# Turning the softmax scores of seven attention tiles by 32x32 blocks and through device memory, in a fused attention, gated-unit and soft-routing kernel

## The chip, the cores and the metric

The kernel runs on one core of a Trainium2 chip. The metric is device microseconds of one launch. Its engines here are PE (TensorE, matrix products), DVE (VectorE), ACT (ScalarE), POOL (GpSimd) and SP (SyncE, which issues the DMAs).

## The reference, cut to what matters

Three parts run behind one another on 4 batches of 576 tokens (2304 tokens, 512 features, 8 heads of 64).

```python
# attention: pooled by 4 (global) plus a band of +-3 keys (local)
scores = where(|i - j| < 4, scale * q @ k.T, -1e9)
attn = exp(scores - max); attn = attn / (sum + 1e-9)
x = out_up + attn @ v
# gated unit, 512 -> 1536 -> 512
h = sigmoid(x @ w_gate) * (x @ w_val);  x2 = h @ w_out
# soft routing: 8 experts with 4 slots each
logits = x2 @ phi
slot_input = softmax(logits, tokens).T @ x2
slot_out[e] = relu(slot_input[e] @ w1[e]) @ w2[e]
out = softmax(logits, slots) @ slot_out
```

All of it is float32. The change touches the step `attn @ v` of the local part.

## The kernel before, in words

The tokens are cut into 18 tiles of 128. Tiles 0 to 15 get their local attention on PE; tiles 16 and 17 get theirs on DVE, ACT and POOL (the functions named z_...), in a stage that opens when the on-chip memory of the first kind is given back.

Local attention of one tile (helpers from line 390 on). A tile is two blocks of 64 queries. `lsq` (L450) makes the scores of 8 heads against 70 keys for both blocks on PE, into two PSUM banks; `lmq` (L465) scales and masks them into the tile `t` (128 partitions by 8 heads by 70 keys); `lx` (L500) takes the maxima; `le` (L506) the exponentials, eight on ACT; `la` and `ln` (L514, L519) divide by the sums on DVE. `lt` (L525) turns the eight 128x70 pieces with eight identity matmuls on PE into two PSUM banks `psT`, and `lc` (L531) copies these on ACT into `pt` (70 partitions). `lo` (L537) makes 16 products of `pt` with the values `lv` on PE into `psO`; `xa` (L551) adds the global part on DVE and `l_split` (L592) splits the result into a high and a low half on ACT and POOL. `pt` has one buffer, `t` and `lv` have two.

The gated unit (`unit`, L874) of a tile has six parts of 256 hidden columns. A part is 12 matmuls of 128x512 into one of two banks `psM`, in two halves of six; ACT takes a tanh and DVE a product (`uh`, L866), which frees the bank. Tile t is worked on after its attention is done, so the attention of later tiles, the global attention and the routing of earlier tiles are laid between the halves.

The order is written by hand in half-slots (`place`, L1196): half-slot h comes after half h of the matmuls, counted from tile 4, with 12 half-slots to a tile. PE runs in this order, exactly. On the other engines, and in SP's queue, the framework orders by its own simulated times; only from half-slot 100 on is DVE held to program order as well. The attention tiles T = 6 to 15 have h = 10(T - 6): scores at h, division at h + 5, turning at h + 7, values at h + 9:

```python
        place(h + 5, lambda T=T: l_norm(T))
        place(h + 7, lambda T=T: (l_tr(T, 0), l_tr(T, 1)))
        place(h + 9, lambda T=T: (l_av(T), l_split(T)))
```

At half-slot 100 `to_band` (L1262) gives back the memory of `t`, `pt`, `lq`, `lk` and `lv`, and the rows of the last two tiles are loaded into it (`token_row`, L611); the products with them (`z_prod`, L636) stand on DVE ahead of the next `uh`.

One thing in the kernel before is already done in the way of the change: for tiles 3 to 11 the hidden values `h` are turned for the routing by `turn` (L900: four DVE transposes of 32x32 blocks, each followed by a DMA to device memory, `hod`) and `move` (L910: four DMAs back, into `hT`), at places 1 and 2 of a tile's 12 half-slots for most tiles.

The expert weights (33 MB) are loaded late, into memory that the gated unit gives back piece by piece (L1041, L1084, L1092 and, at the end, `get2` and `get2p`, L1046 and L1099, under the helper line 136 or L1047).

Of the kernel before, what the change touches and what calls it, by code (L numbers as in the profile page):

```python
# [7 lines left out]
F32 = mybir.dt.float32  # L8
# [7 lines left out]
P = 128  # L16
QB = 64
KW = QB + 6
# [4 lines left out]
def kernel(  # L23
# [16 lines left out]
    nc = tc.nc  # L40
    B, NP, _, SP = qT.shape[0], qT.shape[1], qT.shape[2], kT.shape[3]
# [5 lines left out]
    NTL = NT // P  # L47
    TS = 6
    TB = 16
    FF = wo.shape[0]  # L50
    NC = DM // P
    FU = 256
    NU = FF // FU
    NF = FF // P
    GW = FF // 4
    NE, _, F2 = w1.shape
# [3 lines left out]
    def pool(stack, name, bufs, side=None, space=None):  # L60
        kw = {"space": space} if space is not None else {}
        if side:
            kw["side"] = side
        return stack.enter_context(tc.tile_pool(name=name, bufs=bufs, **kw))
# [10 lines left out]
    sf = pool(dense, "sf", 1)  # L75
# [7 lines left out]
    def bank(pl, tag, name):  # L83
        return pl.tile([P, 512], F32, name=name, tag=tag)
# [9 lines left out]
    mask = sf.tile([P, 3, KW], F32, name="mask")  # L94

    wod = tc.dram_tile([FF, DM], F32, name="wod")
    hod = [tc.dram_tile([4 * P, GW], F32, name=f"hod{i}") for i in range(2)]

    st = {"pin": True, "pe": False, "all": False, "vec": False, "act": False}
# [8 lines left out]
    def tmm(*args, **kw):  # L108
        ins = nc.tensor.matmul(*args, **kw)  # L109
        if st["pe"]:  # L110
            tc.keep_in_program_order(ins)
# [21 lines left out]
    vec, act, gps, syn = Engine(nc.vector, "vec"), Engine(nc.scalar, "act"), Engine(nc.gpsimd, "all"), Engine(nc.sync, "all")  # L133

    def load(dst, src):
        ins = nc.sync.dma_start(dst, src)
        if st["pin"]:
            tc.keep_in_program_order(ins)
# [88 lines left out]
    def copy(alt, dst, src):  # L227
        if alt:
            vec.tensor_copy(out=dst, in_=src)
        else:  # L230
            act.copy(out=dst, in_=src)
# [155 lines left out]
    L = {}  # L387
# [44 lines left out]
    def load_tile(t):  # L432
        if t < NTL:
            load_q(t), load_k(t), load_v(t, 1)
# [15 lines left out]
    def lsq(t):  # L450
        d = L[t]
        for h in range(2):
            d["ps", h] = bank(ps_at, "at", "psS")
        for p in range(NP):
            for j in range(2):
                c = slice(64 * j, 64 * j + 64)
                ko = d["ko"][j]
                for h in range(2):
                    r = slice(64 * h, 64 * h + 64)
                    tmm(  # L460
                        d["ps", h][c, p * KW:(p + 1) * KW], lhsT=d["q"][r, p, j * QB:(j + 1) * QB],
                        rhs=d["k"][r, p, ko:ko + KW], start=True, stop=True, tile_position=(64 * h, 64 * j),
                    )

    def lmq(t, h):  # L465
        d = L[t]
        if "t" not in d:
            d["t"] = sf.tile([P, 2, NP, KW], F32, name="t", tag="t", bufs=2)
        kinds = [0 if i == 0 else (2 if i == NB - 1 else 1) for _, i in blocks(t)]
        rows = [(0, P, kinds[0])] if kinds[0] == kinds[1] else [(64 * j, 64 * j + 64, kinds[j]) for j in range(2)]  # L470
        ps = d.pop(("ps", h))
        for a, b, kind in rows:
            vec.scalar_tensor_tensor(
                out=d["t"][a:b, h],
                in0=ps[a:b, :NP * KW].rearrange("p (b w) -> p b w", w=KW),
                scalar=0.125,
                in1=mask[a:b, kind].unsqueeze(1).to_broadcast([b - a, NP, KW]),
                op0=ALU.mult,
                op1=ALU.add,
            )  # L480
# [16 lines left out]
    def groups(t):  # L497
        return L[t]["t"].rearrange("p j b w -> p (j b) w")

    def lx(t):  # L500
        d = L[t]
        mx = d["mx"] = sm.tile([P, 2 * NP], F32, name="mxl", tag="mxl")
        vec.tensor_reduce(out=mx, in_=groups(t), axis=AX.X, op=ALU.max, negate=True)
        d["sl"] = sm.tile([P, 2 * NP], F32, name="sl", tag="sl")
# [20 lines left out]
    def lt(t, j):  # L525
        d = L[t]
        ps = d["ps", j] = bank(ps_at, "at", "psT")
        for p in range(NP):
            ttr(ps[:KW, p * P:(p + 1) * P], d["t"][:, j, p, :], ident)

    def lc(t, j, alt=False):  # L531
        d = L[t]
        if "pt" not in d:
            d["pt"] = sf.tile([KW, 2, NP, P], F32, name="pt", tag="pt")
        copy(alt, d["pt"][:, j], d.pop(("ps", j))[:KW, :].rearrange("p (b q) -> p b q", q=P))

    def lo(t):  # L537
        d = L[t]
        ps = d["ps"] = bank(ps_at, "at", "psO")
        for j in range(2):  # L540
            for p in range(NP):
                for h in range(2):
                    r, c = slice(64 * h, 64 * h + 64), slice(64 * j, 64 * j + 64)
                    tmm(
                        ps[r, p * P + j * QB:p * P + (j + 1) * QB],
                        lhsT=d["v"][j][:, p * P + 64 * h:p * P + 64 * h + 64],
                        rhs=d["pt"][:, h, p, c] if t >= TS else d["pt"][:, j, p, r],
                        start=True, stop=True,
                    )

    def xa(t):  # L551
        x = new_x(t)
        pv = L[t].pop("ps").rearrange("e (p g r) -> e p g r", p=NP, r=4)
        xv = x.rearrange("e p (g r) -> e p g r", r=4)
        (b0, i0), (b1, i1) = blocks(t)
        if b0 == b1:
            pieces = [(b0, i0 * 16, 0, 32)]
        else:
            pieces = [(b0, i0 * 16, 0, 16), (b1, i1 * 16, 16, 16)]
        for b, o, g, n in pieces:  # L560
            vec.tensor_tensor(
                out=xv[:, :, g:g + n], in0=pv[:, :, g:g + n],
                in1=odb[b][:, :, o:o + n].unsqueeze(3).to_broadcast([P, NP, n, 4]), op=ALU.add,
            )
# [4 lines left out]
    def l_norm(t):  # L569
        la(t), ln(t)  # L570

    def l_tr(t, j):
        lt(t, j), lc(t, j)

    def l_av(t):
        lo(t), xa(t)
# [6 lines left out]
    def to_hi(t):  # L583
        xh[t] = xs.tile([P, NC, P], F32R, name="xh", tag="xh")
        act.copy(out=xh[t], in_=xt[t])

    def to_lo(t, eng):
        xl[t] = xs.tile([P, NC, P], F32R, name="xl", tag="xl")
        eng.tensor_tensor(out=xl[t], in0=xt.pop(t), in1=xh[t].bitcast(F32), op=ALU.subtract)
        L.pop(t, None)  # L590

    def l_split(t):  # L592
        to_hi(t), to_lo(t, gps)
# [6 lines left out]
    def pieces(m):  # L600

        a, r = TB * P + 2 * P * m, []
        while a < TB * P + 2 * P * (m + 1):
            b, o = divmod(a, S)
            n = min(S - o, TB * P + 2 * P * (m + 1) - a)
            p0 = (a - TB * P - 2 * P * m) // 2
            r.append((p0, n // 2, b, o))
# [13 lines left out]
    def z_start(m):  # L621
        d = Z[m] = {}
        ew = st["ew"]
        d["q"] = ew.tile([P, 2, DM], F32, name="zq", tag="zq")
        a = TB * P + 2 * P * m
        load(d["q"], qn[a:a + 2 * P, :].rearrange("(p r) e -> p r e", r=2))
# [86 lines left out]
    def z_rows(m, r):  # L713
        o = Z[m]["o"]
        t = TB + 2 * m + r
        ps = bank(ps_at, "at", "psT")
# [149 lines left out]
    def uh(t, u):  # L866
        if t not in hs:
            hs[t] = hs[t - 3] if TX < t < TY else (st["h5"] if t == K0 else hp).tile([P, FF], F32, name="h", tag="h")
        vec.scalar_tensor_tensor(
# [30 lines left out]
    def turn(t):  # L900
        if "y" not in st:
            st["y"] = hp.tile([P, FF], F32, name="hy", tag="h")
        src = hs[t].rearrange("p (c r w) -> p c r w", r=4, w=32)
# [207 lines left out]
    def pair(k):  # L1111
        if k not in G:
# [6 lines left out]
            out=grp, in_=ident.rearrange("p (g r) -> p g r", r=4), axis=AX.X, op=ALU.add  # L1119
# [76 lines left out]
    def place(at, fn, rank=1):  # L1196
        half_slots.setdefault(at, []).append((rank, len(half_slots.get(at, [])), fn))

    EVERY = 10
    for i, T in enumerate(range(TS, TB)):  # L1200
        h = EVERY * i
        place(
            h, lambda T=T: (load_tile(T + 1) if T + 1 < TB else None, lsq(T), lmq(T, 0), lmq(T, 1))
        )
        place(h + 1, lambda T=T: lx(T))
        for j in range(4):
            place(h + 1 + j, lambda T=T, j=j: le(T, j, 2), 2)
        place(h + 5, lambda T=T: l_norm(T))
        place(h + 7, lambda T=T: (l_tr(T, 0), l_tr(T, 1)))
        place(h + 9, lambda T=T: (l_av(T), l_split(T)))  # L1210
    for i, h in enumerate((10, 20, 45, 62)):
        q = 4 + i
        for a in range(2):
# [41 lines left out]
    for t in range(K0 + 3, TL):  # L1255
        h = HS * (t - K0)
# [30 lines left out]
    for t in range(K0, TL):  # L1287
# [7 lines left out]
        for u in range(NU):  # L1295
            h = HS * (t - K0) + 2 * u
# [69 lines left out]
    for p in PLAN:  # L1366
# [3 lines left out]
        i = "abc".index(p)  # L1370
        t, u = TL + i, un[i]
# [245 lines left out]
    t = 0  # L1617
# [55 lines left out]
```

## Time and profile before

| what | value |
|---|---|
| runs, median of 3 | 541.03 us (540.21 to 541.84) |
| the profiled execution's own time | 541.66 us |
| its span, first to last instruction | 539.9 us |
| busy PE / DVE / ACT / POOL | 509.8 / 289.9 / 225.6 / 93.2 us |
| mean granted clock of TensorE | 0.994 of full speed |
| moved by DMA | 108.57 MB |

The span is 1.8 us shorter than the execution's own time, and the execution is 0.6 us above the median. In the rows further on, times are microseconds from the span's start. A row of the chain gives start, duration and the work that the end of the span goes back to. A row of the timeline gives start, duration, engine, line, operation, output and inputs, and in brackets the idle time of the engine before it. Operations recorded by helpers carry the helper's line (L109 and L114 for PE, L126 for the others, L136 for loads). One float32 product counts as two or more MATMULs in some groups.

### The profile page before, as it was taken

To read this page: it belongs to the slowest core of one execution; us is meant where nothing else is said; L and a number is where in the kernel's file an instruction comes from. 1 tells how busy PE (TensorE), PEld (TensorE's weight loads), DVE (VectorE), ACT (ScalarE), POOL (GpSimd) and SP (SyncE) were. 2 spreads that over 40 slices of the span, in tenths; PEclk is the share of its full clock that TensorE was granted. 3 is DMA by queue.
4 is the path that set the end of the run, shared out by engine and by line. 5 is a ranking of instruction groups with operands and counts; after the bars stand their busy time and mean duration, and the time that the engine had idled before them with its cause. 6 is when DMAs were issued, how large, how long until landed. Compare 5 with 4: busy or idle time off the path is not lost.

```text
span 539.9 us, 11054 instructions
## 1 busy us (share of the span) xinstructions
PE 509.8 (94%) x4218; PEld 375.3 (70%) x4218; DVE 289.9 (54%) x667; ACT 225.6 (42%) x773; POOL 93.2 (17%) x154
## 2 busy tenths in 40 slices
PE   3989999999999999999999999999999999999972
PEld 2566777788877767777777777777777777753431
DVE  6989999888326563645353544458763211241123
ACT  3887646476445443433353442413333212231222
POOL 0210322001344142312220101000284000000000
PEclk9999999999999999999999999999999999999997
DMA  8897665887534557744751514295216666799948
GB/s 305 244 258 266 188 232 191 275 266 240 160 118 118 150 165 218 194 114 126 165 153 48 157 42 118 81 294 191 83 56 254 240 254 227 240 398 343 387 151 333
DMA packets 68332, 108.57 MB, mean 201 GB/s; under 512 B 10744, under 2 KB 32632, under 8 KB 68280
## 3 DMA queue, kind: packets, MB, share of 16 engines
q1 hardware_dynamic: 68280, 107.88, 61.6%
q8 instruction: 33, 0.54, 0.4%
q14 instruction: 19, 0.16, 0.1%
HBM read 92.91 MB, written 14.94 MB: 200 GB/s over the span
## 4 chain that ended last, share of the span: by engine, by line
PE 76%; DMA 11%; DVE 7%; ACT 2%; issue 1%; SPq 1%; DVEq 0%; ACTq 0%
PE psM L109 51%; PE psL L109 6%; DMA ew<-in_w_dram 5%; PE psO L109 4%; DVE wf L126 3%; PE psH L114 2%; PE psS L109 2%; PE psT L114 2%; PE psW L109 2%; PE psD L109 1%; PE psEH L109 1%; DMA g<-in_kT_dram 1%; DMA raw<-in_wg_dram 1%; DMA raw<-in_wv_dram 1%; DMA lv<-in_vp_dram 1%
## 5 line engine op out<-in xcount | busy, mean ns | idle before, releaser
L109 PE MATMUL psM<-whi,xh 128*128 128x512 f32 x432 | 182.8, 423 | 2.0 <-DVE h L126 2.0
L109 PE MATMUL psM<-wlo,xh 128*128 128x512 f32 x432 | 170.6, 395 | 0.0
L109 PE MATMUL psM<-whi,xl 128*128 128x512 f32 x432 | 170.6, 395 | 0.0
L126 ACT ACTIVATE th<-psM 128x256 f32<-128x256 f32 x108 | 41.3, 383 | 155.7 <-PE psM L109 151.8
L109 PEld LDWEIGHTS psM<-whi,xh 128*128 128x128 f32 x432 | 81.5, 189 | 32.1 <-issue 9.8
L126 DVE SCALAR_TENSOR_TENSOR h<-th,psM 128x256 f32<-128x256 f32 x108 | 44.7, 414 | 102.5 <-ACT th L126 102.3
L109 PEld LDWEIGHTS psM<-whi,xl 128*128 128x128 f32 x432 | 81.2, 188 | 19.5
L109 PEld LDWEIGHTS psM<-wlo,xh 128*128 128x128 f32 x432 | 81.6, 189 | 13.7
L126 DVE SCALAR_TENSOR_TENSOR wf<-raw,wf 128x512 uint32<-128x512 uint32 x72 | 48.5, 686 | 0.3
L126 ACT ACTIVATE t<-t,mxl 128x70 f32<-128x70 f32 x128 | 43.4, 348 | 10.9 <-DVE mxl L126 10.9
L126 POOL TENSOR_TENSOR xl<-x,xh 128x512 fp32r<-128x512 f32 x15 | 19.8, 1320 | 129.3 <-ACT xh L126 129.3
L126 ACT ACTIVATE wf<-raw 128x512 f32<-128x512 f32 x36 | 24.3, 676 | 25.8 <-DMA raw<-in_wg_dram 11.1
L126 POOL TENSOR_TENSOR wlo<-wf,whi 128x512 fp32r<-128x512 f32 x10 | 14.8, 1487 | 67.9 <-ACT whi L126 31.1
L126 ACT ACTIVATION_READ_ACCUMULATOR t<-t,mxl 128x1 f32 x128 | 24.9, 194 | 0.0
L126 DVE SCALAR_TENSOR_TENSOR t<-psS,mask 128x280 f32<-128x280 f32 (+1 forms) x38 | 16.0, 443 | 16.5 <-PE psS L109 16.3
L126 ACT COPY hT<-psH 128x512 f32<-128x512 f32 (+1 forms) x29 | 16.1, 556 | 13.5 <-PE psH L114 13.1
L126 ACT CAST xh<-x 128x512 fp32r<-128x512 f32 x18 | 11.2, 623 | 21.3 <-DVE x L126 21.3
L689 POOL TENSOR_TENSOR hy<-hy,prv 128x512 f32<-128x512 f32 x12 | 17.1, 1459 | 7.2 <-PE psM L109 3.8
L109 PEld LDWEIGHTS psO<-pt,lv 70*64 70x64 f32 x448 | 14.2, 138 | 6.0 <-issue 4.3
L126 DVE STREAM_TRANSPOSE hy<-h 128x384 f32<-128x384 f32 x36 | 17.8, 548 | 0.5 <-DMA hod<-hy 0.3
L126 DVE TENSOR_SCALAR wf<-wf 128x512 uint32<-128x512 uint32 x36 | 15.4, 437 | 4.5 <-ACT wf L126 4.4
L109 PE MATMUL psO<-pt,lv 70*64 70x64 f32 x448 | 16.1, 225 | 1.6 <-DMA lv<-in_vp_dram 1.2
(195 smaller groups left out, 693.0 us busy)
## 6 DMA issues: line engine op xcount, KB each, us to landing
ew<-in_w_dram SPq DMA_DIRECT2D x19, 1024.0 KB
hod<-hy SPq DMA_DIRECT2D x36, 192.0 KB
hT<-hod SPq DMA_DIRECT2D x36, 192.0 KB
raw<-in_wg_dram SPq DMA_DIRECT2D x12, 512.0 KB
raw<-in_wv_dram SPq DMA_DIRECT2D x12, 512.0 KB
raw<-in_wo_dram SPq DMA_DIRECT2D x12, 512.0 KB
ewp<-in_w_dram SPq DMA_DIRECT2D x20, 256.0 KB
ewp<-in_w_dram SPq DMA_DIRECT2D x8, 512.0 KB
```

The lines of the kernel that those rows point to most:

```text
L109: ins = nc.tensor.matmul(*args, **kw)
L114: ins = nc.tensor.transpose(*args)
L126: ins = fn(*args, **kw)
L689: nc.gpsimd.tensor_tensor(out=e, in0=e, in1=pr[:, r], op=ALU.add)
```

## The change

For tiles 9 to 15 the eight identity matmuls and the two ACT copies go. In their place stands `l_turn`: three DVE transposes of 32x32 blocks (key columns 0 to 31, 32 to 63 and 38 to 69 of all eight heads, 128x256 elements each), one DMA of the result to device memory (128 rows of 3 KB), and three DMAs back into `pt`, in runs of 1 KB onto 32, 32 and 6 partitions. The result's buffer `py` takes the memory of tile 4's hidden values. `pt` keeps its size but has another layout, so that `lo` reads two runs of 32 columns instead of one of 64. `l_turn` stands at h + 5, right behind the division (tile 9: h + 8), and the values at h + 10 (tile 9: h + 14) instead of h + 9. All of tile 15 comes two half-slots earlier (88 instead of 90), so its values are at 98 instead of 99.

```diff
+    TURNED = (9, 15)
+    pod = [tc.dram_tile([P, 24 * 32], F32, name=f"pod{i}") for i in range(2)]
+    def l_turn(t):
+        d = L[t]
+        if t < 9:
+            y = st["y"]
+        else:
+            if "py" not in st:
+                st["py"] = st["h5"].tile([P, FF], F32, name="py", tag="h")
+            y = st["py"]
+        y = y[:, :24 * 32]
+        yv = y.rearrange("p (k g w) -> p k g w", g=2 * NP, w=32)
+        g = groups(t)
+        vec.transpose(out=yv[:, 0], in_=g[:, :, :32])
+        vec.transpose(out=yv[:, 1], in_=g[:, :, 32:64])
+        vec.transpose(out=yv[:, 2], in_=g[:, :, KW - 32:])
+        m = pod[t % 2]
+        nc.sync.dma_start(m, y)
+        pt = sf.tile([KW, 4, 2 * NP, 32], F32, name="pt", tag="pt")
+        d["pt"] = pt
+        mv = m.rearrange("(a w) (k e) -> k w a e", w=32, k=3)
+        for k, r, w in ((0, 0, 0), (1, 32, 0), (2, 64, 96 - KW)):
+            nc.sync.dma_start(pt[r:r + 32 - w].rearrange("w a g q -> w a (g q)"), mv[k, w:])
...
-                        rhs=d["pt"][:, h, p, c] if t >= TS else d["pt"][:, j, p, r],
+                        rhs=(
+                            d["pt"][:, 2 * j:2 * j + 2, h * NP + p, :] if TURNED[0] <= t <= TURNED[1]
+                            else d["pt"][:, h, p, c] if t >= TS else d["pt"][:, j, p, r]
+                        ),
...
-        h = EVERY * i
+        h = min(EVERY * i, 88)
...
-        place(h + 7, lambda T=T: (l_tr(T, 0), l_tr(T, 1)))
-        place(h + 9, lambda T=T: (l_av(T), l_split(T)))
+        if TURNED[0] <= T <= TURNED[1]:
+            w = h + {7: 10, 8: 8, 9: 8}.get(T, 5)
+            place(w, lambda T=T: l_turn(T))
+            place(h + {7: 14, 8: 12, 9: 14}.get(T, 10), lambda T=T: (l_av(T), l_split(T)))
+        else:
+            place(h + 7, lambda T=T: (l_tr(T, 0), l_tr(T, 1)))
+            place(h + 9, lambda T=T: (l_av(T), l_split(T)))
```

## Rows read from the trace of the kernel before

**Rows 1.** The page: busy time and share of the span by engine.

```profile
PE 509.8 (94%) x4218; PEld 375.3 (70%) x4218; DVE 289.9 (54%) x667; ACT 225.6 (42%) x773; POOL 93.2 (17%) x154
```

**Rows 2.** Busy time by stretch: start:end, length, then PE, PEld, DVE, ACT, POOL, clock, DMA.

```profile
294.00:314.00 20.00, 20.00 (x179) 15.50 (x177) 8.95 (x23) 8.22 (x35) 1.65 (x3) 1.00 0.44 122
...
352.00:373.00 21.00, 20.56 (x147) 15.97 (x143) 13.79 (x22) 4.73 (x14) 1.68 (x3) 1.00 0.80 276
...
480.00:540.00 60.00, 46.26 (x411) 19.33 (x403) 13.92 (x30) 14.49 (x34) 0.53 (x1) 0.94 0.84 312
```

**Rows 3.** The chain in time, 226 to 418 us: start, us, what.

```profile
226.38 0.87 PE psT L114 x8
227.25 1.44 PE psL L109 x32
...
249.77 1.40 PE psM L109 x6
...
252.68 1.08 PE psO L109 x32
253.77 1.59 PE psM L109 x6
...
313.21 1.08 PE psO L109 x32
...
332.62 1.08 PE psO L109 x32
...
348.12 0.87 PE psT L114 x8
...
351.80 1.10 PE psO L109 x32
...
417.16 1.44 PE psL L109 x32
```

**Rows 4.** Instructions on tile psT: duration ns min/median/max, first and last start.

```profile
L114 PE MATMUL psT<-ident,t x128: 270/273/303, 24.7 to 348.7; 128*70 128x128 f32 x128
L126 ACT COPY pt<-psT x29: 566/584/604, 27.3 to 349.1; 70x512 f32<-70x512 f32 x29
```

**Rows 5.** Instructions on tile hy (the turn that is there already), DVE.

```profile
L126 DVE STREAM_TRANSPOSE hy<-h x36: 528/536/579, 180.8 to 347.6; 128x384 f32<-128x384 f32 x36
```

**Rows 6.** The timeline of DVE: the division of tiles 10, 13 and 14.

```profile
240.87 0.73 DVE L126 TENSOR_TENSOR t<-t,sl 128x560 f32<-128x560 f32 x1
...
305.15 0.73 DVE L126 TENSOR_TENSOR t<-t,sl 128x560 f32<-128x560 f32 x1
...
321.91 0.73 DVE L126 TENSOR_TENSOR t<-t,sl 128x560 f32<-128x560 f32 x1
```

**Rows 7.** The timeline of SP's queue, 232 to 352 us.

```profile
246.06 0.35 SPq L136 DMA_DIRECT2D gk<-in_kT_dram  x1
...
303.82 2.39 SPq L914 DMA_DIRECT2D hT<-hod  x4
...
324.66 2.87 SPq L908 DMA_DIRECT2D hod<-hy  x4
328.56 1.75 SPq L914 DMA_DIRECT2D hT<-hod  x4
346.79 1.81 SPq L908 DMA_DIRECT2D hod<-hy  x4
348.74 1.86 SPq L914 DMA_DIRECT2D hT<-hod  x4
```

**Rows 8.** The chain in time, 352 to 359 us: the first rows of tiles 16, 17.

```profile
353.84 4.07 DMA row<-in_kp_dram
...
358.03 0.69 DVE prk L126
```

**Rows 9.** The chain in time, from 494 us on.

```profile
494.22 14.37 DMA ew<-in_w_dram
508.60 11.23 DMA ew<-in_w_dram
```

**Rows 10.** Waits of SP's queue, 400 to 500 us: total us, times, longest.

```profile
SPq L1047 <- PE psM L109: 26.9, 3, 9.5
SPq L1042 <- PE psM L109: 11.3, 3, 7.4
```

## The prediction

> **What bounds the kernel now.** I read the share of each engine first, then the busy time by stretch, then the chain in time through the stretch in which tiles 9 to 15 are turned, then what stands on DVE and in SP's queue there.
>
> PE is busy for 94% of the span [rows 1]. In the stretch that the change touches it has no gap: 20.00 of 20.00 us between 294 and 314, with DVE at 8.95, ACT at 8.22 and the DMA engines at 0.44 [rows 2]. So what leaves PE's order there moves the end, and what is put on DVE, SP and the DMAs is free as long as it is in time. The chain says the same: it passes from psM to psT to psL to psO, all PE, each piece beginning where the last ended [rows 3]. The granted clock is 1.00 in that stretch [rows 2], the upper of the two levels, and stays there, since PE goes on without a pause; I put no term on it.
>
> **The change, part by part.**
>
> *The identity matmuls.* Eight of them hold the chain for 0.87 us; seven tiles have such a piece, of which the first and the last stand in the rows [rows 3]. 7 x 0.87 = 6.1 us less.
>
> One matmul's own duration is 273 ns [rows 4], but eight in 0.87 us are 0.109 us apart: they overlap, and only the distance counts. The Trainium skill, "TensorE: Matmul & The Clock Gate", Part 4: PE-mode transpose, gives about 275 ns for one in a kernel's context; the duration in this trace agrees, but as a price it would make 56 x 0.275 = 15.4 us, which the chain excludes unless the neighbours slow down too.
>
> *The copies.* 14 ACT copies of 0.584 us [rows 4] go. ACT is busy 8.22 of 20 us [rows 2] and nothing on the chain waits for these: no gain.
>
> *The values' operand.* `lo` now reads two runs of 32 columns. The logits have both forms already: those of a turned tile read runs of 32 (1.44 us at 227.25), those of a late tile read 128 in a row (1.44 us at 417.16) [rows 3]. Nothing either way.
>
> *DVE.* Three transposes of 128x256 a tile. The nearest row is 536 ns for 128x384 [rows 5]: between 0.36 (in proportion) and 0.54 (no smaller) each. I take 0.40, near the proportion, so 1.2 us a tile, at most 1.6. Behind them on DVE stands the product `uh`, which frees a psM bank. How long can it be late? At tile 16's first row DVE waited some 4.07 us for a DMA [rows 8], and PE lost 21.00 - 20.56 = 0.44 us in that stretch [rows 2]. Tile 14 is the worst: its l_turn has the same place as the four transposes of tile 10's hidden values. 1.6 + 4 x 0.536 = 3.7 us is still under 4.07. Nothing, then; 0.4 us if a division falls in as well.
>
> *The way through memory, against the time there is.* Turning must be done before `lo`.
> - Write: SP's first reader of `hod` is issued 1.95 us after the first 192 KB write (346.79 to 348.74), in the worst case 3.90 (324.66 to 328.56) [rows 7]. The new write has 384 KB in one DMA. I take 2.5.
> - Reads: three DMAs, 280 KB. From below: 1.95, the same way in the other direction, and two more issues of 0.35 each [rows 7], 2.6. From above: the row loads, with other loads ahead, took 4.2 from first issue to first use (353.84 to 358.03) [rows 8]. I take 3.0, nearer the lower end, as 280 KB is little beside those rows.
> - Sum with DVE's 1.2: 6.7 us; ends 5.6 (1.1 + 1.95 + 2.6) and 9.7 (1.6 + 3.9 + 4.2).
>
> The time there is: from the end of the division to psO of before, less the psT piece (0.87), plus one half-slot more (six matmuls, 1.59 behind other work [rows 3]), so 0.72 more than before. Tile 13: 313.21 + 0.72 - 305.88 = 8.0. Tile 14: 332.62 + 0.72 - 322.64 = 10.7. Tile 10: 252.68 + 0.72 - 241.60 = 11.8 [rows 3, 6]. Tile 9 has six half-slots instead of five between turning and values; tile 15 moves as a whole.
>
> *SP's queue.* Four DMAs more a tile, 28 in all, about 0.35 us each. Reads wait for the write, and what stands behind them waits too: the loads of the next tile but one, not needed for some 20 us, and `hod`'s reads, needed six half-slots later. The danger is the other way round, that the new DMAs stand behind something. Tile 10: `gk` waits for POOL until 246.06 [rows 7]; with the write behind it (246.41 instead of 242.8) the chain is 6.7 + 3.6 = 10.3, under 11.8. Tile 14: the four writes of `hod` take 2.87 us [rows 7], 6.7 + 2.9 = 9.6, under 10.7. Tile 13: the reads into `hT` are issued until 306.19 [rows 7], before the write is ready at 307.1; only their data are still under way. With the chain's upper end, 9.7, the three are late by 1.5 (tile 10), 1.7 (tile 13) and 1.9 (tile 14), 5.1 together. The margins at my values are 1.5, 1.3 and 1.1, so I put 0.7 us on it in all.
>
> *Tile 15 earlier.* Its `lo` comes one half of six matmuls (1.40 [rows 3]) sooner. It frees the memory for the first rows of tiles 16 and 17, whose lateness cost the 0.44 us. I take 0.4 less; ends 0 and 0.44.
>
> **The sum**: 541.66 - 6.1 - 0.4 + 0.7 = 535.9 for the profiled execution, which is 0.6 above the median, so **535.2 us** against 541.03.
>
> **Rivals.**
>
> *Late in a few tiles.* Two or three of tiles 10, 13 and 14 find `pt` not there, 2.5 to 4 us in all instead of 0.7: 537.0 to 538.5. For it: margins of a microsecond beside a chain of two DMAs whose ends lie four apart. Against it: DMAs are at 0.44 there. 17%.
>
> *The end is set by the weights.* The chain's last part is 14.37 + 11.23 us of weight loads [rows 9], with the DMA engines at 0.84 [rows 2]. If those ran from a fixed time, PE's gain would be waited away: 541.0, or 1 us less. Against it: these loads wait for PE to free memory (26.9 us and 11.3 us in SP's queue behind psM [rows 10]), so they start earlier with PE. 9%.
>
> *Turning becomes the bound: slower.* The mechanism is one: `lo` waits on PE for the last read, in every tile. The gain of 6.5 is gone when the seven are late by 0.93 us on average, and the kernel is slower by over 0.3% (1.6 us, about what a measurement of it can tell) from 1.2 us on. With the upper end of the chain and SP held as by `gk` every time, 9.7 + 3.6 = 13.3 against 11.8, 8.0 and 10.7 is 3.1 late on average: 541.0 - 6.5 + 7 x 3.1 = 556. At 2 us each it is 548.5. SP's queue is ordered by simulated times, so a bad place can come in every tile; but for seven of seven the rows give no reason. 11%. The Trainium skill, "VectorE: DVE Perf Modes", Rules for kernel authors, speaks for this one: it gives a 128x128 transpose to TensorE where PSUM will do as its destination, and VectorE's only for work inside 32x32 blocks. No row here shows this kernel the other way.
>
> *Identity matmuls worth their own duration.* 56 x 0.273 = 15.3 us, 526. The chain speaks against it: 1%.
>
> That the change would not do what it says I leave out: the old pieces are gone from the code for all seven tiles.
>
> **How the numbers follow.** The forecast has 62%; its range is 533.0 (the sum with no lateness, 534.5, and 1.5 for a schedule that falls out better) to 537. With the second case it reaches 538.5; up to 540.5 it also takes in half of the third: 62 + 17 + 4 is a little over 8 in 10. Faster: 62 + 17 + 1 = 80%. Within 0.3%: 9%. Slower: 11%.
>
> **What the profile after would show.** psT only for tiles 6 to 8 (besides the head); the chain from psM to psL or psO without the 0.87 us. PE at 20 of 20 us still; a wait of PE's psO for a DMA into `pt` is the forecast's failing point, tile 13 first, then 14 and 10. Three DVE transposes of about 0.4 us a tile; from the write's issue to the first read's 2.5 us. The row wait at tile 16 shorter, and the part from there to the end of the same length: if it is longer by the gain, the weights set the end.

## The result, and the profile after

The changed kernel takes 533.59 us (median of 4 runs, 532.46 to 534.74) against 540.62 for the kernel before (median of 4, 538.92 to 541.84): the ratio is 0.9872, 95% interval 0.9837 to 0.9907, so 5.0 to 8.8 us faster. Measured again, it gave 0.9833 (0.9801 to 0.9864). 535.2 was forecast, in a range from 533.0 to 540.5. Two profiles further on ("the matmuls back" and "the changed kernel again") are of slow executions, 548.90 and 542.15 us, in which the granted clock falls ahead of the stretch that is compared (0.85 between 100 and 150 us), so that their times from the span's start lie some 9 us later; in the stretch itself it is 1.00.

The chain of the changed kernel in time, with the pieces that answer to those of before: start, us, what.

```profile
205.54 0.87 PE psT L116 x8
...
226.46 1.44 PE psL L111 x32
...
239.28 1.08 PE psO L111 x32
240.36 1.44 PE psL L111 x32
...
252.19 1.08 PE psO L111 x32
253.28 0.65 PE psS L111 x32
...
309.55 1.08 PE psO L111 x32
...
343.09 1.08 PE psO L111 x32
344.17 8.79 PE psM L111 x36
352.95 1.44 PE psL L111 x32
```

The last psT is tile 8's. Before, tile 9's psT stood at 226.38 ahead of the same logits [rows 3]; now they follow psM. From tile 8's psT to the logits behind the first rows of tile 16 I take the one stretch by which all kernels are compared. After, it is 352.95 - 205.54 = 147.41 us. Before, it went from

```profile
205.45 0.87 PE psT L114 x8
...
360.76 1.42 PE psL L109 x29
```

which is 155.31: 7.90 less. To the left of it both kernels are alike to 0.1 us. To the right the span has 177.8 us left after and 179.1 before, so nothing of the gain is given back. The two profiled executions differ by 9.2 us (541.66 to 532.46), the medians by 7.0; what the 1.3 us behind the stretch come from was not looked for.

Busy time by stretch, after (start:end, length, PE, PEld, DVE, ACT, POOL, clock, DMA share, GB/s):

```profile
294.00:314.00 20.00, 20.00 (x179) 15.02 (x179) 11.38 (x30) 7.52 (x36) 2.96 (x4) 1.00 0.62 179
...
343.00:364.00 21.00, 21.00 (x148) 16.36 (x148) 14.31 (x22) 4.31 (x13) 2.68 (x3) 1.00 0.92 308
```

PE still has no gap, and the gap of 0.44 us around tile 16's first rows is closed; DVE has more, ACT less [rows 2]. Over the whole stretch PE is busy for 147.41 of 147.41 us; before it was busy for 154.65 of 155.31. No psO of the turned tiles waits for `pt`. What the new work takes, from the instructions on tile py (duration ns min/median/max; the landing is that of one write, tile 15's, the only one the profile gives), the timeline of SP, and SP's waits between 256 and 273 us:

```profile
L128 DVE STREAM_TRANSPOSE py<-t x21: 400/402/446, 228.5 to 332.7; 128x256 f32<-128x256 f32 x21
DMA to landing us min/median/max: 2.3/2.3/2.3
```

```profile
262.18 0.56 SPq L554 DMA_DIRECT2D pod<-py  x1
262.84 2.53 SPq L138 DMA_DIRECT2D gw<-in_vp_dram  x4
265.48 0.52 SPq L138 DMA_DIRECT2D gq<-in_qT_dram  x1
268.49 1.19 SPq L559 DMA_DIRECT2D pt<-pod  x3
...
302.88 0.34 SPq L554 DMA_DIRECT2D pod<-py  x1
306.00 1.17 SPq L559 DMA_DIRECT2D pt<-pod  x3
```

```profile
SPq L559 <- DMA pod<-py: 2.5, 1, 2.5
```

The second pair is tile 13's: 3.1 us from the write's issue to the first read's. The last read is issued 0.8 us later and a read lands 2.4 us after its issue (median over the reads of 128 KB whose landing the profile gives), so `pt` is there at about 309.2 (an estimate), and psO begins at 309.55: 0.3 us to spare. The first pair is tile 11's: its reads are issued 6.3 us after the write and land at about 271.7 for a psO at 272.07. Five loads of the global attention stand between, but they are issued by 266.0; for the last 2.5 us SP waits for the write itself, which lands only at about 268.5. The DMA engines are at 0.74 to 0.92 between 262 and 268 us. That the loads slow the write is likely, and not shown by itself.

### The profile page after: what moved, and what is told of

The parts are those of the page before. It is cut to its first block, busy times and chain, and to the rows that moved or that the text cites. A ratio compares the mean times of both kernels' runs of the same rounds, so it can differ in the third digit from the quotient of the medians.

```text
span 530.7 us, 11003 instructions
## 1 busy us (share of the span) xinstructions
PE 501.1 (94%) x4162; PEld 369.5 (70%) x4162; DVE 297.9 (56%) x688; ACT 218.6 (41%) x759; POOL 93.4 (18%) x154
## 4 chain that ended last, share of the span: by engine, by line
PE 78%; DMA 11%; DVE 5%; ACT 2%; issue 1%; SPq 1%; ACTq 0%; DVEq 0%
PE psM L111 53%; PE psL L111 6%; DMA ew<-in_w_dram 5%; PE psO L111 4%; DVE wf L128 2%; DMA g<-in_kT_dram 2%; PE psH L116 2%; PE psS L111 2%; PE psW L111 2%; PE psD L111 1%; PE psEH L111 1%; DMA raw<-in_wv_dram 1%; DMA raw<-in_wg_dram 1%; PE psF L111 1%; DMA lv<-in_vp_dram 1%
```

## The experiments

All times are of the stretch defined above, from one profile each, unless it says otherwise; ratios are to the kernel before, measured beside it.

**The places without the turning.** The kernel before, with:

```diff
-        h = EVERY * i
+        h = min(EVERY * i, 88)
...
-        place(h + 9, lambda T=T: (l_av(T), l_split(T)))
+        place(h + {9: 14}.get(T, 10 if T > 9 else 9), lambda T=T: (l_av(T), l_split(T)))
```

> The kernel before with its identity matmuls, but with the values of tiles 9 to 15 at the places of the changed kernel and tile 15 two half-slots earlier. Measured in the stretch from tile 8's psT to the logits behind tile 16's first rows: 155.3 us before, 147.4 after, 7.9 less. Theory 'three terms' (matmuls 6.1, row wait 0.4, and about 1.2 because the values of tiles 10 to 14 now stand directly ahead of the next tile's scores, so PE changes between kinds of work less often): 153.5 to 153.9, and 1.4 to 1.8 us off the whole time. Rival 'matmuls alone' (the matmuls are worth all but the row wait): 154.9, 0.4 off.

Measured: 205.44 to 359.70, 154.26, so 1.05 less, and 0.9963 (0.9937 to 0.9989) of the time. Most of it is not the row wait, which is still there (the waits of PE, total us, times, longest):

```profile
PE psM L109 <- DVE h L126: 0.3, 1, 0.3
PE psL L114 <- ACT cexp L126: 0.2, 1, 0.2
```

The wait for `h` was 0.44 before, so 0.9 of the 1.05 us come from the places. The pieces of the chain say which: tiles 10 to 13, whose psO now stands directly ahead of psS, gain 0.7 together, and tile 9, whose psO now stands directly ahead of the logits, 0.2. Tile 14 gains nothing, since tile 15's scores have moved ahead of its values. Between the two theories, nearer to the three terms: the number falls short of 153.5 to 153.9 by the waits that stayed.

**Tile 15 alone.** The kernel before with the first of these two edits.

> The kernel before with tile 15 two half-slots earlier and nothing else. Both theories: the wait for tile 16's first rows goes, 0.4 us off the stretch (154.9 of 155.3). Rival: the rows come no earlier against PE, 155.3.

Measured: 203.57 to 358.17, 154.60, so 0.71 less; 0.9973 (0.9942 to 1.0004) of the time, which by itself is not clear of noise. At the rows PE runs through:

```profile
347.09 1.08 PE psO L109 x32
348.17 9.99 PE psM L109 x42
358.17 1.44 PE psL L109 x32
```

The wait was worth 0.7 us and not the 0.44 of its gap. The kernel before shows why: the six matmuls after the gap take 1.66 us and not 1.40:

```profile
358.72 0.34 DVE h L126
359.06 0.04 issue
359.11 1.66 PE psM L109 x6
```

**The matmuls back.** The changed kernel, with:

```diff
+            place(h + 7, lambda T=T: (lt(T, 0), lt(T, 1)))
             place(h + {7: 14, 8: 12, 9: 14}.get(T, 10), lambda T=T: (l_av(T), l_split(T)))
```

> The changed kernel with the 56 identity matmuls issued again at h + 7 into banks that nobody reads; the turning through memory stays. Theory 'three terms': 7 x 0.87 = 6.1 us back, the stretch at 153.5, the time near 539.7. Rival 'matmuls alone': 7.0 to 7.5 back, 154.4 to 154.9.

Measured: 214.78 to 368.18, 153.40, which is 5.99 over the changed kernel; 0.9978 (0.9958 to 0.9998) of the kernel before. Seven pieces of 0.87 us stand in the chain again, 6.1: that was the right price, and the rival with 7.0 falls. So does a price of 273 ns for each. The ratios, 0.9978 against 0.9872 without the matmuls, say the same: some 5.7 us of the whole time. The 5.99 also hold a small difference at tile 16's rows. There the 36 matmuls behind tile 15's psO take

```profile
359.58 8.59 PE psM L111 x36
```

and in the changed kernel 8.79: 0.2 us of the row wait is still in that kernel, without a gap that the profile shows.

**No way through memory.** The changed kernel with `l_turn` cut down to:

```diff
+        if "pt" not in st:
+            st["pt"] = sf.tile([KW, 4, 2 * NP, 32], F32, name="pt", tag="pt")
+            gps.memset(st["pt"], 0.01)
+        d["pt"] = st["pt"]
```

> The changed kernel without the 21 DVE transposes and the 28 DMAs: pt is filled once with a constant, so the local part of tiles 9 to 15 is left out of the result. Theory 'the way through memory is hidden at no cost': the stretch stays at 147.4 (within 0.2) and the time within 0.3%. Rival 'it costs a little on DVE and in SP's queue': 0.5 to 1.5 us faster.

Measured: 203.60 to 352.02, 148.42; 0.9842 (0.9791 to 0.9894). It is no faster than the changed kernel; it is 1.0 slower in the stretch, and that is the row wait come back:

```profile
PE psM L111 <- DVE h L128: 0.9, 1, 0.9
```

Without that gap, 147.5, as in the changed kernel. The 21 transposes and 28 DMAs cost nothing. The stretch is outside the 0.2 us that were expected, because of the rows. Where the rows hang is seen in SP's queue:

```profile
338.42 2.46 SPq L920 DMA_DIRECT2D hod<-hy  x4
340.99 1.85 SPq L926 DMA_DIRECT2D hT<-hod  x4
342.94 0.38 SPq L138 DMA_DIRECT2D bm<-in_cst_dram  x1
343.37 0.42 SPq L138 DMA_DIRECT2D zq<-in_qn_dram  x1
343.85 1.37 SPq L138 DMA_DIRECT2D row<-in_kp_dram  x3
```

The row loads stand behind the reads of tile 11's hidden values, which in turn wait for their writes. It is the same in the changed kernel, but there the four writes are issued in less time:

```profile
340.36 1.80 SPq L935 DMA_DIRECT2D hod<-hy  x4
```

Memory that comes free earlier brings the rows forward only as far as that. From the first row load's issue to the first product with it, 5.4 us pass here (343.85 to 349.29) and 5.0 there (345.21 to 350.22); whether PE is made to wait hangs on these tenths.

**Values one half-slot earlier**, and **two**. The changed kernel, with `10` replaced by `9` or `8` in:

```diff
-            place(h + {7: 14, 8: 12, 9: 14}.get(T, 10), lambda T=T: (l_av(T), l_split(T)))
+            place(h + {7: 14, 8: 12, 9: 14}.get(T, 9), lambda T=T: (l_av(T), l_split(T)))
```

> The changed kernel with the values of tiles 10 to 15 one half-slot earlier, at h + 9. Theory: the last read of pt lands 2.4 us after its issue, which leaves 0.3 us ahead of psO in tiles 11 and 13 and over 1 us elsewhere, so with 1.4 to 1.6 us less both make PE wait, 1.1 to 1.3 each, and the direct neighbourhood with the scores is lost, 1.0: the stretch at 150.5 to 151.0. Rival 'there is more room than the landing shows': no wait, 148.4.

Measured at h + 9: 206.20 to 356.74, 150.54, so 3.1 more; 0.9884 (0.9856 to 0.9911). The waits of PE:

```profile
PE psO L111 <- DMA pt<-pod: 1.5, 2, 0.9
PE psM L111 <- DVE h L128: 0.7, 1, 0.7
```

PE waits 1.5 us for `pt`, in the two tiles that were named but for less in each, and 0.7 at the rows. Most of the remaining 0.9 is the neighbourhood that tiles 10 to 13 lost, 0.7 in the first experiment. The rival falls.

> The changed kernel with the values of tiles 10 to 15 two half-slots earlier, at h + 8. Theory: PE waits for pt in nearly every tile, 2.5 to 3.2 us in tiles 11 and 13 and 0 to 2 in the others; in all 7 to 12 us, the stretch at 155 to 160, so the gain is gone or turned round. Rival: waits in tiles 11 and 13 only, 153 to 154.

Measured at h + 8: 205.44 to 361.49, 156.05; 1.0015 (0.9988 to 1.0043), no gain left. PE waits 5.7 us for `pt` in four tiles; tiles 11 and 13:

```profile
270.46 1.15 PE L111 MATMUL psO<-pt,lv 70*64 70x64 f32 x32 [1.54 <-DMA pt<-pod]
...
313.06 1.15 PE L111 MATMUL psO<-pt,lv 70*64 70x64 f32 x32 [2.27 <-DMA pt<-pod]
```

Less in each than expected, 5.7 in all, but the stretch is 8.6 longer. 0.65 of that is the row wait, and some 1.6 come behind tile 11's wait: the granted clock falls to 0.50 there, the lower level, and the pieces that follow take 0.99 and 2.64 us where such pieces behind a psO took 0.56 and 1.48 (at tile 9 before). By stretch, and the chain:

```profile
268.00:270.40 2.40, 0.92 (x4) 0.39 (x3) 0.39 (x1) 0.00 (x0) 1.55 (x4) 1.00 0.52 163
...
272.00:274.00 2.00, 2.00 (x8) 1.71 (x8) 0.97 (x4) 1.29 (x5) 0.86 (x1) 0.50 0.44 120
```

```profile
271.61 0.99 PE psL L111 x4
272.60 2.64 PE psM L111 x6
```

So the point from which the change is worth nothing lies two half-slots from where it stands.

**The change for more tiles.** `TURNED = (8, 15)` and `TURNED = (7, 15)`.

> The change for tiles 8 to 15. Tile 8 shares its buffer with the turn of the hidden values. Theory: another 0.87 us off, the time near 532.7, if the shared buffer makes nobody wait. Rival: DVE or SP waits for that buffer and tile 8's pt is late: no gain or a loss of 1 to 2 us.

Measured: 0.9955 (0.9926 to 0.9984), 540.32 us: worse than the changed kernel's 0.9872 or 0.9833. The rival is right about the buffer, not about tile 8's `pt`, which is in time, and the loss is larger than it said. The place is plain. SP's queue and DVE (in brackets the idle time before):

```profile
198.93 4.43 SPq L138 DMA_DIRECT2D gk<-in_kT_dram  x2
203.45 0.38 SPq L554 DMA_DIRECT2D pod<-hy  x1
```

```profile
197.61 1.10 DVE L128 STREAM_TRANSPOSE hy<-t 128x256 f32<-128x256 f32 x3
...
207.26 1.04 DVE L128 STREAM_TRANSPOSE hy<-h 128x384 f32<-128x384 f32 x2 [4.80 <-DMA pod<-hy]
```

Tile 8's block transposes are done at 198.7, but their write waits in the queue behind a load that waits for POOL. Until the write has landed DVE may not put the hidden values into the same buffer, stands still for 4.80 us, and PE waits:

```profile
PE psL L116 <- ACT cexp L128: 3.8, 1, 3.8
```

Here too the granted clock falls to 0.50, and the next twelve matmuls take 5.12 us where they take 2.80 elsewhere. One thing more is in this profile: tile 13, at its old place, waits for `pt`.

```profile
315.73 1.15 PE L111 MATMUL psO<-pt,lv 70*64 70x64 f32 x32 [0.49 <-DMA pt<-pod]
```

Its reads are issued 3.9 us after its write (308.57 to 312.47) and not 3.1 as in the changed kernel. So the 0.3 us that it has to spare there are gone when the write takes 0.8 us longer.

> The change for tiles 7 to 15. Theory: 1.7 us off the changed kernel, near 531.9. Rival: the stretch of tile 7 and 8 has more loads in SP's queue (those of the global attention) and the shared buffer, so pt is late and the time is 533 or more.

Measured: 536.3 us, 0.989 (0.9866 to 0.9914). No gain over the changed kernel. The shared buffer is again in the way: DVE stands still for 2.85 us until the write out of it has landed, PE waits 2.5 us for DVE, and the granted clock is at 0.50 between 190 and 196 us. `pt` is late in tile 13 alone, by 0.5 us. A buffer of its own for tile 8 was not tried.

**More tiles beside their neighbours.** The changed kernel with `h + 9` of the tiles that still have matmuls set to `h + 10`.

> The changed kernel, with the values of tiles 6, 7 and 8 (still turned by identity matmuls) also at h + 10, directly ahead of the next tile's scores. Theory 'changes of work cost PE time': about 0.2 us for each of the three, so the way from tile 6's scores to the logits behind tile 16's first rows is 209.4 to 209.9 instead of 210.1 us. Rival 'their places are neutral': 210.1.

Measured from tile 6's scores to the logits: 141.62 to 353.85, 212.2 us, against 142.83 to 352.95, 210.1, in the changed kernel; 0.987 (0.9839 to 0.9902). Neither theory: 2.1 us are lost, because other waits begin (1.7 us more of them). Tile 6's values, tile 7's scores and the global scores now come together, and the chain runs through DVE and ACT instead of PE from 163.3 to 173.7. The largest new wait of PE:

```profile
PE psL L116 <- ACT cexp L128: 1.4, 1, 1.4
```

**The changed kernel again.**

> The changed kernel once more, to have the experiments of the other calls beside it: the same stretch at 147.4 to 147.5 us from tile 8's psT, no wait of psO for pt, and 5.5 to 7.5 us less than the kernel before.

Measured: 533.68 us, 0.9833 (0.9801 to 0.9864), by the medians of all runs 8.4 less than the 542.05 of the kernel before beside it, where 5.5 to 7.5 was expected. In its profile the stretch is 214.42 to 362.44, 148.02, 0.6 more than in the first, most of it the row wait, 0.4 by its gap:

```profile
PE psM L111 <- DVE h L128: 0.4, 1, 0.4
```

The rest is at tile 11, whose psO begins 0.07 us late:

```profile
280.96 0.07 issue
281.03 1.15 PE psO L111 x32
```

The view names nobody that it waited for, but 1.15 us is what psO took behind a wait for `pt` at h + 9 and h + 8, and 1.08 to 1.11 otherwise. So in two executions of one program `pt` is in time in the one and just about so in the other, and the rows are late by 0.2 and by 0.7 us.

## Why the prediction was right, point by point

*What bounds the kernel*: right. PE had gaps of 0.66 us in 155 before and has none after, and the 7.9 us gained in the stretch are still there at the end.

*The identity matmuls, 6.1 us*: right, 5.99 by putting them back, 6.2 when the 0.2 at the rows are set apart.

*The values' operand*: right, psO takes 1.08 us with either layout.

*DVE, 0.40 us a transpose and nothing on the path*: right, 402 ns; leaving them out gains nothing. The 4.07 us that served as a bound were the row DMA's own time; DVE was idle for 4.35 us there, and PE lost 0.70 and not 0.44.

*The way through memory, 6.7 us*: too short. Tile 13 takes some 7.5 (301.76 to 309.2): the write to the first read was put at 2.5 and took 3.1, the reads at 3.0 and took about 3.2. The time there was, 8.0 by the prediction, was 7.8 (301.72 to 309.55). It lay inside the ends that were given, and *the allowance of 0.7 us for lateness* was not needed: no wait for `pt` in one profile and some 0.1 us in the other. That it was not needed is in part luck: with 0.3 us to spare, 0.5 us of waiting came with tiles 7 or 8 turned as well, and 1.5 at one half-slot less.

*SP's queue*: half right. Tiles 10, 13 and 14 were named; tile 11, for which nothing was worked out, had as little to spare as tile 13. What held it was not a place in the queue but the write itself, which landed some 6 us after its issue beside the loads of the global attention, where the worst case was put at 3.9. The danger named, new DMAs behind a load that waits for POOL, came with tile 8, where the change does not reach.

*Tile 15, 0.4 us*: undersized. 0.7 by itself, as a gap on PE also costs the slow start after it, and 0.5 in the changed kernel, where 0.2 stay; and not sure, since the rows hang on another DMA of the queue, which the step did not look at.

*What was left out*: that the new place of the values is a gain. The sum moved them one half-slot back and counted that as time for `pt`; it did not ask what stands beside them there. psO directly ahead of psS saves PE the way back to psM and out again: the six matmuls after psO take 1.59 and not 1.40 [rows 3]. Tiles 10 to 13 gain 0.7 us by it, and tile 9 gains 0.2 in the same way ahead of the logits, 0.9 in all by the first experiment. And the copies were taken for no gain: a wait of PE for ACT of 0.2 us is there in the first experiment, where ACT copies psT, and not with the matmuls back, where nobody does.

By the runs: 6.2 for the matmuls, 0.9 for the places, 0.5 for the rows, 0.2 for ACT, together 7.8 of 7.9; the sum had 5.8. The forecast was too high by its allowance and by the two terms that it lacked. *The rivals*: lateness in a few tiles and turning as the bound begin at h + 9 and h + 8; at h + 10 tile 13 was late by 0.5 us in two kernels with more tiles turned, and in neither run of this one. The end is not set by the weights.

The Trainium skill ("VectorE: DVE Perf Modes", Rules for kernel authors) gives a 128x128 transpose to TensorE where PSUM will do as its destination. For the 128x70 pieces of this kernel the measurement says otherwise: VectorE with two steps through memory is the faster way, 533.6 against 540.6 us, since TensorE is the bound. The 275 ns that the Trainium skill gives for one transpose ("TensorE: Matmul & The Clock Gate", Part 4: PE-mode transpose) are no price here either: in the chain one costs 0.109 us.

## What to carry to other kernels

Where PE is the bound without a gap, work that leaves its order is worth its share of the chain (0.87 us for eight transposes), not its instructions' durations, and a detour of 7.5 us through two DMAs is free as long as it ends before the place in PE's order that needs it. Compute that room for every tile with what stands in the DMA queue there, and measure it by moving the consumer: here one place less costs 3.1 us, two 8.6. Leave more room than 0.3 us: the same write held its reads for 3.1 us in one of these kernels and for 3.9 in another. When work is moved in such an order, price its new neighbours too, and don't let a buffer of the new path be shared with a writer that cannot wait.

## What was not expected of the hardware

A piece of other work between PE's long matmuls costs more than itself: the six after psO take 1.59 us and not 1.40, the six after a wait 1.66. A wait of PE can cost more than its length: behind 1.5 us of waiting in tile 11 at h + 8, and behind 3.8 with tile 8 turned, the granted clock stood at 0.50 for some 3 to 5 us; behind 2.3 us in tile 13 of the first of these kernels it stayed at 1.00. What makes the difference stays open. And the time of a DMA depended less on its size than on where in the kernel it stood: in the changed kernel 384 KB written as one DMA landed 2.3 us after its issue in tile 15, and a read of 128 KB 2.4 us after, but the same write held its reads for 3.1 us in tile 13 and for 6.3 in tile 11.
